# Crossbar transposes, a lag of three blocks and a new VectorE order in a windowed-attention and highway kernel

## Chip, cores, metric

One core of one Trainium2 chip. The metric is the device time of one execution in microseconds; each kernel is run several times and the fast runs are compared. A "span" in a profile is the time from the first to the last instruction and is some 1.7 to 2.4 us shorter than the device time of the same run.

## The reference

Four sequences of 768 tokens, eight heads of 64: every query attends to the 128 last positions and to the first four ("sinks"). The result, as 3072 tokens of 512 features, goes through a highway layer.

```python
keep = (pos[None, :] < 4) | ((rel >= 0) & (rel < 128))
scores = np.where(keep, q @ k.T / 8, -1e9)
x = softmax(scores) @ v                       # [3072, 512]
H = np.maximum(x @ w_h, 0.0)
T = 1.0 / (1.0 + np.exp(-(x @ w_t + b_t)))
out = T * H + (1.0 - T) * x
```

## The kernel before

It works in 24 blocks of 128 tokens, six to a sequence (a "batch" below). Per block TensorE makes transposes of q and k (`tp`), window scores (`sps`), attention output (`av`), transposes of x (`xtp`) and the two highway products (`tps`, `hps`). Once in two blocks it makes sink scores (`sk`). ScalarE does the exponentials (`e`, `es`), copies and the tanh (`u`). VectorE multiplies the masks in (`e`), and does `kT`, `rec`, `xh` (x, normalised), `dd`, `ee`, `otok`. All q, k and v loads are issued by GpSimd and cast fp32 to fp16 on the way. (`dd`, `ee`, `otok` are the three steps of the highway sum; PSUM, below, is the memory that TensorE writes its results to, HBM the memory off the cores.)

```python
AHEAD = 8
x_pool  = tile_pool(name="p_x", bufs=4)
av_ps   = tile_pool(name="ps_av", bufs=1, space=PSUM)
m_ps    = tile_pool(name="ps_m", bufs=2, space=PSUM)   # tp, sk, tps and hps share these two
...
def stage_T(n):                          # q, k of block n to [feature, token]
    ...
    nc.scalar.copy(out=qT, in_=tp[:, 0:NHP, :])
    nc.vector.tensor_copy(out=kT, in_=tp[:, NHP:2 * NHP, :])
def stage_sink_setup(b):                 # once a batch: ten small SBUF-to-SBUF copies
    for hh in range(2):
        nc.sync.dma_start(out=ks3[...], in_=kT[rows, :, 0:NSINK])
    for h in range(H):
        nc.sync.dma_start(out=vs_bd[b % 2][r:r + NSINK, ...], in_=vt[0:NSINK, ...])
def stage_X(n):
    xtp = av_ps.tile([P, NOC, P], FP16, tag="av")
    for j in range(NOC):
        nc.tensor.transpose(xtp[:, j, :], xh[:, 2 * j:2 * j + 2, :], ident)
    nc.scalar.copy(out=xT, in_=xtp)
...
for i in range(-2, NB + 1):              # cut to its order; s = i + 1
    stage_sink(i)                        # blocks 2 and 4 of a batch
    stage_S(s); stage_A(i)               # scores of the next block; av, rec, xh
    stage_T(i + 2); stage_sink_setup(...)
    load(i + 2 + AHEAD); load_v(i + 2 + AHEAD)      # GpSimd's queue
    stage_mask(s)
    stage_Mt(i - 1); stage_X(i)
    stage_Mh(i - 1)                      # hps, then dd, ee, otok one after the other
```

The softmax here doesn't subtract the row's maximum and nothing guards it: scores larger than these inputs give would overflow.

## Time and profile before

| | before |
|---|---|
| device time, median of 3 | 136.59 us |
| VectorE busy, whole span | 108.5 us (80%) |
| one batch of six blocks, steady | 28.1 us |
| last q, k or v load issued | about 80 us |
| q, k loads, issue to landing, median | 7.3 to 7.4 us |

A line of the profile's first page: busy microseconds, share of the span and instructions of each engine (PE is TensorE, PEld its weight loads, DVE VectorE, ACT ScalarE, POOL GpSimd).

```profile
PE 117.1 (87%) x1312; PEld 73.6 (55%) x1312; DVE 108.5 (80%) x230; ACT 90.4 (67%) x129; POOL 65.7 (49%) x81
```

The windows view, one row for each of two batches. Its columns are the stretch and its length, then the busy time and instruction count of TensorE, its weight loads, VectorE, ScalarE and GpSimd, then granted clock, DMA share and GB/s.

```profile
24.20:52.50 28.30, 27.21 (x330) 17.54 (x329) 25.79 (x48) 22.18 (x32) 24.70 (x29) 1.00 2.28 173
52.50:80.60 28.10, 27.01 (x330) 17.37 (x328) 25.83 (x49) 22.18 (x32) 21.64 (x25) 1.00 2.09 189
```

VectorE is busy 92% of such a stretch. The chain of waits shows what that means in one block (start, length, what):

```profile
43.46 0.70 DVE dd L313
...
44.26 0.70 DVE ee L316
...
44.98 0.69 DVE otok L319
45.67 0.13 DVE rec L275
...
45.83 0.69 DVE xh L277
46.52 0.38 DVE kT L186
46.89 1.20 DVE e L247 x2
48.09 0.62 DVE dd L313
```

From dd to dd it is VectorE alone, 4.6 us. Operations that wait for their predecessor (dd to ee, 0.80 us start to start) cost more than independent ones (the two masks, 0.60 each).

The xh of blocks 6, 12, 18 (left out here) and 23 in the timeline of VectorE (start, duration, engine, line, operation, out<-in):

```profile
45.83 0.69 DVE L277 TENSOR_TENSOR xh<-av,rec 128x512 f16<-128x512 f32 x1
73.95 0.69 DVE L277 TENSOR_TENSOR xh<-av,rec 128x512 f16<-128x512 f32 x1
...
125.14 0.69 DVE L277 TENSOR_TENSOR xh<-av,rec 128x512 f16<-128x512 f32 x1
```

A batch is 28.1 us (73.95 - 45.83); after the last block's xh come 9.8 us of drain (134.9 - 125.14).

### The profile page before, as it was taken

The numbers are of one execution on the slowest core, as the hardware profiler recorded it, in microseconds if no ns is written. First come the engines' busy times: TensorE is split into PE (matmuls) and PEld (weight loads), VectorE is DVE, ScalarE is ACT, GpSimd is POOL, SyncE is SP. The second block draws the span as 40 slices with busy tenths as digits, with TensorE's granted clock in tenths as the row PEclk, the third lists the DMA queues.
The fourth block names the chain that finished last, engine by engine and source line by source line (L and its number), as shares of the span: only waits on it lengthen the run. The fifth ranks groups of instructions, "written<-read, shape, count | busy, mean of one in ns | idle before, by whom it ended". The sixth has DMA issues, their size and how long they took to land.

```text
span 134.9 us, 3378 instructions
## 1 busy us (share of the span) xinstructions
PE 117.1 (87%) x1312; PEld 73.6 (55%) x1312; DVE 108.5 (80%) x230; ACT 90.4 (67%) x129; POOL 65.7 (49%) x81
## 2 busy tenths in 40 slices
PE   6657939999999899999999899999998999999720
PEld 2225625856864466567565557656653685665300
DVE  6153724789988999899898998998989998999590
ACT  3054843779775977977777788779767977973310
POOL 6999747889897789979489370000000000000000
PEclk9999995999999999999999999999999999999996
DMA  0999999999999999999999999122011101101111
GB/s 4 111 123 127 160 188 160 155 181 171 154 198 191 196 151 148 152 195 240 192 194 179 193 194 176 38 80 80 6 78 78 63 19 78 78 5 78 78 78 78
DMA packets 81841, 17.02 MB, mean 126 GB/s; under 512 B 77729, under 2 KB 78753, under 8 KB 81826
## 3 DMA queue, kind: packets, MB, share of 16 engines
q0 software_dynamic: 75936, 10.49, 116.0%
q1 hardware_dynamic: 5890, 6.33, 14.6%
q8 instruction: 10, 0.16, 0.5%
q14 instruction: 5, 0.04, 0.1%
HBM read 20.97 MB, written 6.29 MB: 202 GB/s over the span
## 4 chain that ended last, share of the span: by engine, by line
DVE 33%; PE 32%; ACT 11%; issue 8%; POOL 7%; DMA 6%; DVEq 0%; POOLq 0%
PE hps L310 12%; ACT e L234 7%; DMA ksd<-in_k_dram 6%; DVE ee L316 6%; DVE otok L319 6%; DVE dd L313 6%; DVE e L247 5%; DVE xh L277 5%; PE tps L298 4%; PE xtp L286 4%; PE av L262 3%; DVE kT L186 3%; PE sk L211 3%; ACT qT L185 3%; POOL qsd L83 2%
## 5 line engine op out<-in xcount | busy, mean ns | idle before, releaser
L234 ACT ACTIVATE e<-sps,ebias 128x1024 f16<-128x1024 f32 (+1 forms) x48 | 47.4, 1039 | 11.2 <-PE sps L231 6.0
L298 PE MATMUL tps<-wt_sb,xT 128*128 128x512 f16 x96 | 25.5, 390 | 0.0
L310 PE MATMUL hps<-wh_sb,xT 128*128 128x512 f16 x96 | 24.7, 379 | 0.7
L83 POOL DMA_DIRECT2D qsd<-in_q_dram x24 | 21.6, 900 | 4.7 <-DMA wh_sb<-in_moe_w_h_dram 1.0
L84 POOL DMA_DIRECT2D ksd<-in_k_dram x24 | 21.4, 893 | 3.1 <-PE tp L182 1.3
L262 PEld LDWEIGHTS <-e 128*128 128x128 f16 x352 | 19.8, 98 | 3.2 <-issue 0.4
L301 ACT ACTIVATE u<-tps 128x512 f16<-128x512 f32 x24 | 14.4, 600 | 9.5 <-PE tps L298 9.5
L247 DVE TENSOR_TENSOR e<-e,mask 128x1024 f16<-128x1024 f16 x32 | 20.5, 682 | 0.0
L185 ACT COPY qT<-tp 128x512 f16<-128x512 f16 x24 | 14.0, 585 | 9.6 <-PE tp L182 9.6
L313 DVE SCALAR_TENSOR_TENSOR dd<-hps,xh 128x512 f16<-128x512 f32 x24 | 16.5, 688 | 4.1 <-PE hps L310 4.1
L186 DVE COPY kT<-tp 128x512 f16<-128x512 f16 x24 | 10.1, 423 | 11.7 <-ACT qT L185 11.7
L316 DVE SCALAR_TENSOR_TENSOR ee<-u,dd 128x512 f16<-128x512 f16 x24 | 16.6, 692 | 2.5
L319 DVE SCALAR_TENSOR_TENSOR otok<-xh,ee 128x512 f32<-128x512 f16 x24 | 16.6, 692 | 0.8
L277 DVE TENSOR_TENSOR xh<-av,rec 128x512 f16<-128x512 f32 x24 | 16.6, 691 | 0.8
L231 PE MATMUL sps<-qT,kT 64*128 64x128 f16 x352 | 15.4, 227 | 2.1 <-DVE kT L186 1.1
L231 PEld LDWEIGHTS <-kT 64*128 64x128 f16 x352 | 10.7, 98 | 9.5 <-issue 6.6
L288 ACT COPY xT<-xtp 128x512 f16<-128x512 f16 x24 | 14.0, 583 | 1.1 <-PE xtp L286 0.9
L298 PEld LDWEIGHTS <-xT 128*128 128x128 f16 x96 | 9.6, 100 | 9.1 <-issue 0.8
L310 PEld LDWEIGHTS <-xT 128*128 128x128 f16 x96 | 9.3, 98 | 8.6 <-issue 1.5
L286 PEld LDWEIGHTS <-xh 128*128 128x128 f16 x96 | 6.4, 101 | 13.4 <-DVE xh L277 11.2
L286 PE MATMUL xtp<-ident,xh 128*128 128x128 f16 x96 | 9.9, 228 | 3.8 <-DVE xh L277 3.8
L180 PE MATMUL tp<-ident,qsd 128*128 128x128 f16 x96 | 10.0, 231 | 2.4 <-DMA qsd<-in_q_dram 2.3
(88 smaller groups left out, 152.9 us busy)
## 6 DMA issues: line engine op xcount, KB each, us to landing
out_dram<-otok SPq DMA_DIRECT2D x24, 256.0 KB
qsd<-in_q_dram POOLq DMA_DIRECT2D x24, 128.0 KB, 7.3
ksd<-in_k_dram POOLq DMA_DIRECT2D x24, 128.0 KB, 7.4
wt_sb<-in_moe_w_t_dram POOLq DMA_DIRECT2D x1, 512.0 KB, 8.4
wh_sb<-in_moe_w_h_dram POOLq DMA_DIRECT2D x1, 512.0 KB, 10.1
v_91<-in_v_dram POOLq DMA_DIRECT2D x3, 128.0 KB, 8.0
v_92<-in_v_dram POOLq DMA_DIRECT2D x3, 128.0 KB, 6.1
v_93<-in_v_dram POOLq DMA_DIRECT2D x2, 128.0 KB, 8.0
```

Of the source, the lines that this page charges most:

```text
L83: nc.gpsimd.dma_start(out=qsd, in_=q[b, :, rows, :].transpose([1, 0, 2]))
L231: nc.tensor.matmul(sps[:, hh, o:o + P], lhsT=kk[rows, hp, :], rhs=qT[rows, hp, :], start=True, stop=True)
L234: nc.scalar.activation(out=e.rearrange("p a b c d -> p a (b c d)"), in_=sps[:, :, 0:2 * np_ * P], func=AF.Exp, bias=ebias, scale=SCALE)
L247: nc.vector.tensor_tensor(out=ev, in0=ev, in1=m.unsqueeze(1).to_broadcast([P, 4, np_ * P]), op=ALU.mult)
L262: nc.tensor.matmul(av[:, g, 2 * hl + hh, 0:_AVN], lhsT=es[g][:, hh, hl, pc, :], rhs=vt[:, 65 * h:65 * h + _AVN], start=first, stop=False, ...
L277: nc.vector.tensor_tensor(out=xh, in0=avh[:, :, 0:D], in1=rec.unsqueeze(2).to_broadcast([P, H, D]), op=ALU.mult)
L286: nc.tensor.transpose(xtp[:, j, :], xh[:, 2 * j:2 * j + 2, :], ident)
L298: nc.tensor.matmul(tps, lhsT=xT[:, kc, :], rhs=wt_sb[:, kc, :], start=False, stop=(kc == NOC - 1))
L310: nc.tensor.matmul(hps, lhsT=xT[:, kc, :], rhs=wh_sb[:, kc, :], start=(kc == 0), stop=(kc == NOC - 1))
L313: nc.vector.scalar_tensor_tensor(out=dd, in0=hps, scalar=0.0, in1=xh, op0=ALU.max, op1=ALU.subtract)
L316: nc.vector.scalar_tensor_tensor(out=ee, in0=u, scalar=1.0, in1=dd, op0=ALU.add, op1=ALU.mult)
L319: nc.vector.scalar_tensor_tensor(out=otok, in0=xh, scalar=2.0, in1=ee, op0=ALU.mult, op1=ALU.add)
```

## The change

Its intent is to relieve the two busiest engines. x is transposed by the DMA crossbar instead of TensorE and ScalarE, so the highway layer runs three blocks behind to hide the transfer. The kT copy moves to ScalarE, as part of one copy of q and k. VectorE's operations are interleaved so that none directly follows one that it needs. The ten small sink copies become two VectorE copies, one product on VectorE, and one small load by GpSimd, straight from v in HBM.

```diff
-    x_pool = ... bufs=4;  td_pool = ... bufs=3;  NV = AHEAD + 3
+    x_pool = ... bufs=7;  td_pool = ... bufs=4;  NV = AHEAD + 4
-        nc.scalar.copy(out=qT, in_=tp[:, 0:NHP, :])
-        nc.vector.tensor_copy(out=kT, in_=tp[:, NHP:2 * NHP, :])
+        nc.scalar.copy(out=qk, in_=tp)
+    def load_sinks(b):
+        nc.gpsimd.dma_start(out=vs_c[b % 2][:, 0:D], in_=v[b, :, 0:4, :])
     def stage_sink_setup(b):
-        (ten nc.sync.dma_start of ks and vs)
+        nc.vector.tensor_copy(out=ks3[...], in_=kT[rows, :, 0:NSINK])      # twice
+        nc.vector.tensor_tensor(out=vs_bd[...], in0=vs_c[b % 2]..., in1=bdm..., op=ALU.mult)
     def stage_X(n):
-        (four nc.tensor.transpose and a nc.scalar.copy)
+        nc.sync.dma_start_transpose(out=xT, in_=xh.rearrange("p h d -> p (h d)"))
+    LAG = 3
+        for i in range(-2, NB + LAG + 1):        # s = i + 1, m = i - LAG
+            stage_sink(i); stage_S(s); stage_exp(s, 0); stage_T(i + 2); stage_T_copy(i + 2)
+            if (i + 2) % NSC == 0: load_sinks((i + 2) // NSC)
+            load(i + 2 + AHEAD); load_v(i + 2 + AHEAD)
+            stage_exp(s, 1)
+            stage_dd(m - 1); stage_mask(i, 1); stage_ee(m - 1); stage_mask(s, 0)
+            stage_Mt(m); stage_A(i)              # A: av, rec
+            stage_out(m - 1); stage_xh(i); stage_X(i)
+            if i % NSC == 0: stage_sink_setup(i // NSC)
+            stage_Mh(m)
```

(Conditions at the ends of the loop are cut.)

More of the change, by code (lines that the diff above doesn't have):

```diff
@@ L66 @@
     r_pool = ctx.enter_context(tc.tile_pool(name="p_r", bufs=3))
-    x_pool = ctx.enter_context(tc.tile_pool(name="p_x", bufs=4))
-    td_pool = ctx.enter_context(tc.tile_pool(name="p_td", bufs=3))
+    x_pool = ctx.enter_context(tc.tile_pool(name="p_x", bufs=7))
+    td_pool = ctx.enter_context(tc.tile_pool(name="p_td", bufs=4))
     o_pool = ctx.enter_context(tc.tile_pool(name="p_o", bufs=4))
@@ L72 @@
     m_ps = ctx.enter_context(tc.tile_pool(name="ps_m", bufs=2, space=bass.MemoryType.PSUM))
-    NV = AHEAD + 3
+    NV = AHEAD + 4
     v_ring = [const.tile([P, VW], FP16, tag=f"v{i}", name=f"v{i}") for i in range(NV)]
@@ L111 @@
     wt_sb = const.tile([P, NOC, DM], FP16, tag="wt")
+    bdm = const.tile([P, H], FP32, tag="bdm")
+    nc.vector.memset(bdm, 1.0)
     with tc.manual_schedule(engines={ENG.Pool}):
@@ L132 @@
         nc.gpsimd.dma_start(out=wh_sb, in_=moe_w_h.rearrange("(kc p) of -> p kc of", p=P))
+        nc.gpsimd.affine_select(
+            out=bdm, in_=bdm, compare_op=ALU.is_ge, fill=0.0,
+            base=0, pattern=[[-4, H]], channel_multiplier=1)
+        nc.gpsimd.affine_select(
+            out=bdm, in_=bdm, compare_op=ALU.is_ge, fill=0.0,
+            base=NSINK - 1, pattern=[[4, H]], channel_multiplier=-1)
     bt32 = const.tile([1, DM], FP32, tag="bt32")
@@ L143 @@
     mask1 = const.tile([P, 2, P], FP16, tag="mask1", name="mask1")
-    ks_bd, vs_bd = [], []
+    ks_bd, vs_c, vs_bd = [], [], []
     for i in range(2):
-        t = const.tile([P, NHP * 160], FP16, tag=f"ks{i}", name=f"ks{i}")
+        t = const.tile([P, NHP * 136], FP16, tag=f"ks{i}", name=f"ks{i}")
         nc.vector.memset(t, 0.0)
         ks_bd.append(t)
+        t = const.tile([4 * H, 65], FP16, tag=f"vc{i}", name=f"vc{i}")
+        nc.vector.memset(t[:, D:D + 1], 2.0)
+        vs_c.append(t)
         t = const.tile([P, 2, 4, 65], FP16, tag=f"vs{i}", name=f"vs{i}")
@@ L170 @@
     qkT = {}
+    tp_of = {}
+    sps_of = {}
     e_of = {}
     es_of = {}
+    av_of = {}
+    dd_of = {}
+    ee_of = {}
+    hps_of = {}
     xh_of = {}
@@ L182, in stage_T, with stage_T_copy @@
             nc.tensor.transpose(tp[:, NHP + j, :], ksd[:, 2 * j:2 * j + 2, :], ident)
-        qT = qkT_pool.tile([P, NHP, P], FP16, tag="qT", name="qT")
-        kT = qkT_pool.tile([P, NHP, P], FP16, tag="kT", name="kT")
-        nc.scalar.copy(out=qT, in_=tp[:, 0:NHP, :])
-        nc.vector.tensor_copy(out=kT, in_=tp[:, NHP:2 * NHP, :])
-        qkT[n] = (qT, kT)
+        qk = qkT_pool.tile([P, 2 * NHP, P], FP16, tag="qkT", name="qkT")
+        qkT[n] = (qk[:, 0:NHP, :], qk[:, NHP:2 * NHP, :])
+        tp_of[n] = (qk, tp)
+    def stage_T_copy(n):
+        qk, tp = tp_of.pop(n)
+        nc.scalar.copy(out=qk, in_=tp)
+    def load_sinks(b):
+        nc.gpsimd.dma_start(out=vs_c[b % 2][:, 0:D], in_=v[b, :, 0:4, :])
     def stage_sink_setup(b):
         _, kT = qkT[b * NSC]
-        ks3 = ks_bd[b % 2].rearrange("p (a b) -> p a b", b=160)
+        ks3 = ks_bd[b % 2].rearrange("p (a b) -> p a b", b=136)
         for hh in range(2):
             rows = slice(64 * hh, 64 * hh + 64)
-            nc.sync.dma_start(out=ks3[rows, :, 4 * hh:4 * hh + NSINK],
-                              in_=kT[rows, :, 0:NSINK])
-        vt = v_ring[(b * NSC) % NV]
-        for h in range(H):
-            r = 32 * (h // 2) + 4 * (h % 2)
-            nc.sync.dma_start(out=vs_bd[b % 2][r:r + NSINK, h // 4, h % 4, :],
-                              in_=vt[0:NSINK, 65 * h:65 * h + 65])
+            nc.vector.tensor_copy(out=ks3[rows, :, 4 * hh:4 * hh + NSINK],
+                                  in_=kT[rows, :, 0:NSINK])
+        nc.vector.tensor_tensor(
+            out=vs_bd[b % 2][0:4 * H].rearrange("p g h e -> p (g h) e"),
+            in0=vs_c[b % 2].unsqueeze(1).to_broadcast([4 * H, H, 65]),
+            in1=bdm[0:4 * H].unsqueeze(2).to_broadcast([4 * H, H, 65]), op=ALU.mult)
     def stage_sink(n):
@@ L222, in stage_S @@
         es = []
+        sps_of[n] = []
         for g in range(2):
@@ L232, in stage_S, with stage_exp, stage_mask @@
                                          rhs=qT[rows, hp, :], start=True, stop=True)
-            e = e_pool.tile([P, 2, 2, np_, P], FP16, tag="e", name="e")
-            nc.scalar.activation(out=e.rearrange("p a b c d -> p a (b c d)"),
-                                 in_=sps[:, :, 0:2 * np_ * P], func=AF.Exp,
-                                 bias=ebias, scale=SCALE)
-            es.append(e)
-        e_of[n] = (es, np_)
-    def stage_mask(n):
+            sps_of[n].append(sps)
+            es.append(e_pool.tile([P, 2, 2, np_, P], FP16, tag="e", name="e"))
+        e_of[n] = (es, np_)
+    def stage_exp(n, g):
+        es, np_ = e_of[n]
+        nc.scalar.activation(out=es[g].rearrange("p a b c d -> p a (b c d)"),
+                             in_=sps_of[n][g][:, :, 0:2 * np_ * P], func=AF.Exp,
+                             bias=ebias, scale=SCALE)
+    def stage_mask(n, g):
         c = n % NSC
@@ L244, in stage_mask @@
             c, mask.rearrange("p a b -> p (a b)"))
-        for e in es:
-            ev = e.rearrange("p a b c d -> p (a b) (c d)")
-            nc.vector.tensor_tensor(
-                out=ev, in0=ev, in1=m.unsqueeze(1).to_broadcast([P, 4, np_ * P]),
-                op=ALU.mult)
+        ev = es[g].rearrange("p a b c d -> p (a b) (c d)")
+        nc.vector.tensor_tensor(
+            out=ev, in0=ev, in1=m.unsqueeze(1).to_broadcast([P, 4, np_ * P]),
+            op=ALU.mult)
     def stage_A(n):
@@ L275, in stage_A, with stage_xh @@
         nc.vector.reciprocal(out=rec.unsqueeze(2), in_=avh[:, :, 64:65])
+        av_of[n] = (avh, rec)
+    def stage_xh(n):
+        avh, rec = av_of.pop(n)
         xh = x_pool.tile([P, H, D], FP16, tag="xh", name="xh")
@@ L283, in stage_X @@
         xh = xh_of[n]
-        xtp = av_ps.tile([P, NOC, P], FP16, tag="av", name="xtp")
-        for j in range(NOC):
-            nc.tensor.transpose(xtp[:, j, :], xh[:, 2 * j:2 * j + 2, :], ident)
         xT = x_pool.tile([P, NOC, P], FP16, tag="xT", name="xT")
-        nc.scalar.copy(out=xT, in_=xtp)
+        nc.sync.dma_start_transpose(out=xT, in_=xh.rearrange("p h d -> p (h d)"))
         xT_of[n] = xT
@@ L305, in stage_Mh @@
         xT = xT_of.pop(n)
-        xh = xh_of.pop(n).rearrange("p h d -> p (h d)")
-        u = u_of.pop(n)
         hps = m_ps.tile([P, DM], FP32, tag="m", name="hps")
@@ L311, in stage_Mh, with x_flat, stage_dd, stage_ee @@
                              start=(kc == 0), stop=(kc == NOC - 1))
+        hps_of[n] = hps
+    def x_flat(n):
+        return xh_of[n].rearrange("p h d -> p (h d)")
+    def stage_dd(n):
         dd = td_pool.tile([P, DM], FP16, tag="dd", name="dd")
-        nc.vector.scalar_tensor_tensor(out=dd, in0=hps, scalar=0.0, in1=xh,
+        nc.vector.scalar_tensor_tensor(out=dd, in0=hps_of.pop(n), scalar=0.0, in1=x_flat(n),
                                        op0=ALU.max, op1=ALU.subtract)
+        dd_of[n] = dd
+    def stage_ee(n):
         ee = td_pool.tile([P, DM], FP16, tag="ee", name="ee")
-        nc.vector.scalar_tensor_tensor(out=ee, in0=u, scalar=1.0, in1=dd,
+        nc.vector.scalar_tensor_tensor(out=ee, in0=u_of.pop(n), scalar=1.0, in1=dd_of.pop(n),
                                        op0=ALU.add, op1=ALU.mult)
+        ee_of[n] = ee
+    def stage_out(n):
         otok = o_pool.tile([P, DM], FP32, tag="otok", name="otok")
-        nc.vector.scalar_tensor_tensor(out=otok, in0=xh, scalar=2.0, in1=ee,
+        nc.vector.scalar_tensor_tensor(out=otok, in0=x_flat(n), scalar=2.0, in1=ee_of.pop(n),
                                        op0=ALU.mult, op1=ALU.add)
+        del xh_of[n]
         nc.sync.dma_start(out=out[n * P:(n + 1) * P, :], in_=otok)
+    LAG = 3
+    def done(n):
+        return 0 <= n < NB
     with tc.manual_schedule(engines={ENG.PE, ENG.DVE, ENG.Activation}):
-        for i in range(-2, NB + 1):
-            s = i + 1
-            if 0 <= i < NB and i % NSC >= 2 and i % 2 == 0:
+        for i in range(-2, NB + LAG + 1):
+            s, m = i + 1, i - LAG
+            if done(i) and i % NSC >= 2 and i % 2 == 0:
                 stage_sink(i)
-            if 0 <= s < NB:
+            if done(s):
                 stage_S(s)
-            if 0 <= i < NB:
-                stage_A(i)
+                stage_exp(s, 0)
             if i == -2:
@@ L335 @@
                 stage_T(i + 2)
+                stage_T_copy(i + 2)
                 if (i + 2) % NSC == 0:
-                    stage_sink_setup((i + 2) // NSC)
+                    load_sinks((i + 2) // NSC)
             if i == -2:
@@ L346 @@
                     load_v(n)
-            if 0 <= s < NB:
-                stage_mask(s)
-            if 0 <= i - 1 < NB:
-                stage_Mt(i - 1)
-            if 0 <= i < NB:
+            if done(s):
+                stage_exp(s, 1)
+            if done(m - 1):
+                stage_dd(m - 1)
+            if done(i):
+                stage_mask(i, 1)
+            if done(m - 1):
+                stage_ee(m - 1)
+            if done(s):
+                stage_mask(s, 0)
+            if done(m):
+                stage_Mt(m)
+            if done(i):
+                stage_A(i)
+            if done(m - 1):
+                stage_out(m - 1)
+            if done(i):
+                stage_xh(i)
                 stage_X(i)
-            if 0 <= i - 1 < NB:
-                stage_Mh(i - 1)
+            if done(i) and i % NSC == 0:
+                stage_sink_setup(i // NSC)
+            if done(m):
+                stage_Mh(m)
 _INS = ['q', 'k', 'v', 'n_sink', 'window', 'moe_w_h', 'moe_w_t', 'moe_b_t']
```

## The prediction

> **What bounds it now.** In the timeline, a batch of six blocks takes 28.1 us (24.2 to 52.5 us, 52.5 to 80.6, 80.6 to 108.8). VectorE is busy 92% there, the matmul row 96%, ScalarE 78%. The chain of waits alternates between two kinds of block. In one, VectorE goes round without a gap in 4.55 us (43.46 to 48.01): dd, ee, otok, rec, xh, kT, two masks; an operation that depends on the previous one starts up to 0.11 us after its end, an independent one starts 0.08 us before it (0.61 apart instead of 0.72 to 0.80). In the other, with sink scores, hps, sk, es, both exps, qT and kT follow each other in about 5 us. Loads keep the DMA engines full to 84 us but run ahead of use.
>
> **What the change does, per block.** VectorE loses the kT copy (0.42 us) and the dependent gaps: dd, mask, ee, mask, rec, otok, xh at independent distances come to 3.8 us (was 4.55), plus about 0.8 us once a batch for the sinks (was ten small DMAs). TensorE loses the x transposes (0.34 to 0.40 us). ScalarE swaps two 0.58 us copies for one of 1024 columns, about 1.0 us by the page's per-column slope. SyncE gains 24 crossbar transposes of 128 KB.
>
> **How much is on the path.** By engine time TensorE would need about 4.2 us a block, so 10% looks possible. I expect less, because the order creates a new ring. The matmul PSUM pool has two buffers. In the changed kernel's listing tps waits in every steady block for VectorE: it takes the buffer of the previous hps, which dd now frees only after rec, otok and xh. Ring, from durations of before: start of av to rec 1.24 (1.0 without sinks), rec 0.12, otok 0.61, xh 0.61, dd 0.69, wake-up 0.06, tps five matmuls 1.08: 4.41 us. Where a sink stage comes in, tp waits for es in the same buffer: about 4.6. After a batch's first block the sink set-up lies inside the ring: about 4.6. Sum 26.8 us a batch against 28.1, minus 5%, some 4 us over three batches. The first six blocks wait for loads either way (gain about 0). The drain grows by about 2.5 us: three highway blocks remain after the last av instead of one, plus a transpose landing. Net span 133 to 135 against 134.9.
>
> **DMA.** Between xh and its tps lie about 9.7 us. The Trainium skill, "VectorE: DVE Perf Modes", section The three transpose paths, gives 1309 ns for one 128x128 crossbar transpose against 390 on TensorE; no trace here shows one yet. Four make about 5 us (estimate from that page), beside loads that themselves take 7.3 us to land. I expect it to fit.
>
> **Predicted: 135.6 us, 8 in 10 between 130.5 and 143. Faster by over 2%: 0.30; within: 0.45; slower: 0.25.**
>
> **Right or wrong in the profile.** Right: VectorE near 95 us busy; steady batches near 26.8 us; the chain of waits runs av, rec, otok, xh, dd, tps and back; tps waits for dd; VectorE idles before rec. Wrong: if batches take 25 us, the ring is shorter than I think; if TensorE waits for xT, the transposes land too late.
>
> **What would make it wrong.** Transposes above 9.7 us in the loaded stage, or slowing the loads so that tp waits for them (slower). A ring that overlaps more than I sum, giving TensorE's 4.2 us a block: about 128 us.

## The result, and the profile after

| | before | changed |
|---|---|---|
| device time, median | 136.72 us (4 runs) | 152.17 us (4 runs, 150.82 to 153.11) |
| ratio of fast runs | | 1.110 (95%: 1.101 to 1.120) |
| span of the profiled run | 134.9 us | 151.4 us |

A ratio, here and below, is the mean time of one kernel's fast runs over that of the other's of the same rounds, so it is not quite the ratio of the medians. The profiled run of the changed kernel counts as slow (1.5% above its fastest run); the reading below does not rest on that, since fast runs of later kernels (e3, e6) show the same kind of wait.

First page and windows view of the changed kernel, the same lines as above (the stretches are the gap, and the batch of blocks 12 to 17):

```profile
PE 111.8 (74%) x1216; PEld 71.6 (47%) x1216; DVE 98.8 (65%) x223; ACT 87.0 (57%) x105; POOL 68.5 (45%) x87
```
```profile
47.20:63.00 15.80, 0.67 (x12) 0.51 (x9) 0.38 (x4) 2.97 (x3) 9.29 (x11) 0.65 2.46 154
92.40:119.00 26.60, 24.98 (x302) 16.44 (x302) 23.07 (x47) 21.29 (x28) 1.46 (x2) 1.00 0.95 131
```

TensorE, VectorE and ScalarE have less work than before (GpSimd slightly more), and the batch of blocks 12 to 17 takes 26.6 us instead of 28.1. But from 47.2 to 63.0 us TensorE and VectorE do almost nothing. The waits view (who waited for whom: total, times, longest) names it:

```profile
PE tps L322 <- DVE dd L343: 19.5, 6, 16.4
DVE vs_169 L220 <- DMA vc_167<-in_v_dram: 15.4, 1, 15.4
DVE vs_163 L220 <- DMA vc_161<-in_v_dram: 7.5, 1, 7.5
```

And the timelines of VectorE and, below it, of GpSimd give the reason:

```profile
46.61 0.69 DVE L306 TENSOR_TENSOR xh<-av,rec 128x512 f16<-128x512 f32 x1
47.22 0.34 DVE L218 COPY ks_165<-qkT 64x16 f16<-64x16 f16 x2
62.96 0.69 DVE L220 TENSOR_TENSOR vs_169<-vc_167,bdm 32x520 f16<-32x520 f16 x1 [15.40 <-DMA vc_167<-in_v_dram]
```
```profile
53.56 0.88 POOL L84 DMA_DIRECT2D ksd<-in_k_dram  x1 [3.35 <-DMA v_101<-in_v_dram]
54.42 0.89 POOL L91 DMA_DIRECT2D v_92<-in_v_dram  x1
56.62 0.58 POOL L210 DMA_DIRECT2D vc_167<-in_v_dram  x1 [1.31 <-DMA ksd<-in_k_dram]
```

VectorE, which also works strictly in order, reaches the sink product of block 6 at 47.6 us. Its operand `vc_167` is 4 KB, but the instruction that fetches it stands in GpSimd's queue behind the loads of blocks up to 13 (`v_92` is the v of block 13), because the program loads eight blocks ahead. GpSimd, which itself waits for earlier loads on the way (the brackets), gets there at 56.62 us and the bytes land at 62.9. Nothing behind the product can run: no dd, hence no tps, hence no av. TensorE also comes out of the gap at a lower granted clock: 0.65 on average in the gap, 0.50 from 63 to 66 us, 0.63 from 66 to 70 and 1.00 from 70 us on. The four products of the first tps after the gap take 1.71 us in the chain of waits, those of the next 0.86.

The xh lines of blocks 6, 12, 18 and 23:

```profile
46.61 0.69 DVE L306 TENSOR_TENSOR xh<-av,rec 128x512 f16<-128x512 f32 x1
90.80 0.68 DVE L306 TENSOR_TENSOR xh<-av,rec 128x512 f16<-128x512 f32 x1
117.36 0.68 DVE L306 TENSOR_TENSOR xh<-av,rec 128x512 f16<-128x512 f32 x1
138.82 0.68 DVE L306 TENSOR_TENSOR xh<-av,rec 128x512 f16<-128x512 f32 x1
```

One batch takes 44.2 us, the next 26.6. So 17.6 us are lost in one place, 15.4 of them in the wait and some 2 in the slow restart, and the change gains 1.5 us in an undisturbed batch.

### The profile page after: what moved, and what is told of

It reads as the page before. It is cut to its first block, busy times and chain, and to the rows that moved or that the text cites. A ratio compares the mean times of both kernels' runs of the same rounds, so it can differ in the third digit from the quotient of the medians.

```text
span 151.4 us, 3124 instructions
## 1 busy us (share of the span) xinstructions
PE 111.8 (74%) x1216; PEld 71.6 (47%) x1216; DVE 98.8 (65%) x223; ACT 87.0 (57%) x105; POOL 68.5 (45%) x87
## 4 chain that ended last, share of the span: by engine, by line
PE 42%; DVE 23%; DMA 19%; POOL 8%; issue 4%; ACT 1%; DVEq 0%; POOLq 0%
PE tps L324 11%; PE av L287 10%; DMA ksd<-in_k_dram 9%; DVE otok L355 7%; DVE dd L343 6%; DMA vc_161<-in_v_dram 6%; DVE xh L306 5%; PE hps L334 4%; DMA vc_167<-in_v_dram 4%; PE tps L322 4%; PE sps L254 3%; POOL qsd L83 3%; PE sk L233 3%; POOL ksd L84 2%; PE av L293 2%
## 5 line engine op out<-in xcount | busy, mean ns | idle before, releaser
L262 ACT ACTIVATE e<-sps,ebias 128x1024 f16<-128x1024 f32 (+1 forms) x48 | 50.0, 1048 | 9.1 <-PE sps L254 9.0
L207 ACT COPY qkT<-tp 128x1024 f16<-128x1024 f16 x24 | 24.2, 1009 | 10.3 <-PE tp L200 10.3
L287 PEld LDWEIGHTS <-e 128*128 128x128 f16 x352 | 22.9, 103 | 9.8 <-DVE e L272 4.3
L322 PE MATMUL tps<-bt_152,ones_row 128*128 128x512 f16 x24 | 9.3, 386 | 20.1 <-DVE dd L343 19.5
L272 DVE TENSOR_TENSOR e<-e,mask 128x1024 f16<-128x1024 f16 x32 | 21.9, 684 | 1.6 <-ACT e L262 1.3
L254 PE MATMUL sps<-qkT 64*128 64x128 f16 x352 | 16.0, 231 | 3.7 <-ACT qkT L207 2.6
L254 PEld LDWEIGHTS <-qkT 64*128 64x128 f16 x352 | 11.3, 100 | 10.8 <-issue 8.7
L300 DVE RECIPROCAL rec<-av 128x8 f32<-128x8 f32 x24 | 5.0, 208 | 16.3 <-PE av L293 11.8
L236 ACT ACTIVATE es<-sk,ebias 128x256 f16<-128x256 f32 x8 | 3.8, 474 | 13.4 <-PE sk L233 13.4
L220 DVE TENSOR_TENSOR vs_169<-vc_167,bdm 32x520 f16<-32x520 f16 x2 | 1.4, 688 | 15.4 <-DMA vc_167<-in_v_dram 15.4
```

What stands on the lines that cost most here:

```text
L207: nc.scalar.copy(out=qk, in_=tp)
L254: nc.tensor.matmul(sps[:, hh, o:o + P], lhsT=kk[rows, hp, :], rhs=qT[rows, hp, :], start=True, stop=True)
L262: nc.scalar.activation(out=es[g].rearrange("p a b c d -> p a (b c d)"), in_=sps_of[n][g][:, :, 0:2 * np_ * P], func=AF.Exp, bias=ebias, sc ...
L272: nc.vector.tensor_tensor(out=ev, in0=ev, in1=m.unsqueeze(1).to_broadcast([P, 4, np_ * P]), op=ALU.mult)
L287: nc.tensor.matmul(av[:, g, 2 * hl + hh, 0:_AVN], lhsT=es[g][:, hh, hl, pc, :], rhs=vt[:, 65 * h:65 * h + _AVN], start=first, stop=False, ...
```

## The experiments

Two theories at this point. **Queue**: the place of the small load in GpSimd's in-order queue is the cause. **Crossbar**: the transposes slow the big loads (GpSimd reached the v of block 13 at 54.4 us, the kernel before at 46.0), and the sink wait was only where that showed first. Each of these experiments also ran the kernel before on the same chip; e1 to e4 share one set of it (median 136.54 us), e5 to e8 another (137.47). All results were correct.

| run | what | median us | ratio to before (95%) |
|---|---|---|---|
| e1 | sink loads early, by SyncE | 134.98 | 0.989 (0.982 to 0.995) |
| e2 | e1, x transposed on TensorE | 137.20 | 1.006 (0.998 to 1.013) |
| e3 | changed kernel, x transposed on TensorE | 145.42 | 1.064 (1.056 to 1.072) |
| e4 | e1, otok moved out of the ring | 131.34 | 0.960 (0.950 to 0.969) |
| e5 | before, plus dead crossbar transposes | 146.49 | none (3 of 4 runs slow) |
| e6 | before, with the sink values of the change | 143.99 | 1.045 (1.040 to 1.049) |
| e7 | changed kernel, sink loads early, by GpSimd | 138.50 | 1.007 (1.002 to 1.011) |
| e8 | e4, first 8 blocks transposed on TensorE | 130.42 | 0.948 (0.944 to 0.953) |

### e1: the sink loads first, on SyncE

```diff
-        nc.gpsimd.dma_start(out=vs_c[b % 2][:, 0:D], in_=v[b, :, 0:4, :])   # in the loop
+    for b in range(B):                                                      # before the loop
+        t = const.tile([4 * H, 65], FP32, tag=f"vc{b}", name=f"vc{b}")
+        nc.vector.memset(t[:, D:D + 1], 2.0)
+        nc.sync.dma_start(out=t[:, 0:D], in_=v[b, :, 0:4, :])
```

(Cut: the product then reads `vs_c[b]` instead of `vs_c[b % 2]`.)

Expected: 

> Changed kernel, but the four small sink-value loads are issued by SyncE at the very start, in fp32 (VectorE reads them as fp32), instead of by GpSimd among the big loads. Theory Q (queue position): VectorE's waits of 15.4 us and 7.5 us for the sink values are the whole loss, because each small load stood in GpSimd's in-order queue behind the loads of blocks far ahead. Then no such wait is left, the batches take 26.6 us from the first on (as between 92.5 and 119.0 us of the changed kernel), and the time is 152.2 - 16.1 - 2.7 = about 133.5 us (131 to 136.5). Theory X (crossbar): the transposes make the q, k and v loads slow, and the sink wait was only where it showed; then TensorE waits for qsd, ksd or xT instead, and the time stays above 142 us.

Measured: 134.98 us, and no wait for the sink values in the waits view. The xh lines of blocks 6, 12, 18 and 23, from VectorE's timeline of e1:

```profile
45.91 0.68 DVE L306 TENSOR_TENSOR xh<-av,rec 128x512 f16<-128x512 f32 x1
72.48 0.68 DVE L306 TENSOR_TENSOR xh<-av,rec 128x512 f16<-128x512 f32 x1
99.04 0.68 DVE L306 TENSOR_TENSOR xh<-av,rec 128x512 f16<-128x512 f32 x1
120.48 0.68 DVE L306 TENSOR_TENSOR xh<-av,rec 128x512 f16<-128x512 f32 x1
```

Both batches take 26.6 us. The Queue theory holds, the Crossbar theory as stated falls: the crossbar is still there. Only the sink loads were changed (place, engine and type; e7 separates these), and 17 us came back. The first wait, of 7.5 us in block 0, was worth little: block 6's xh came only 0.7 us earlier, because the first blocks wait for their q and k anyway.

### e2: e1 without the crossbar

```diff
-        nc.sync.dma_start_transpose(out=xT, in_=xh...)        # at the end of block i
+        (four nc.tensor.transpose into av_ps, nc.scalar.copy) # after the scores of block i + 2
```

Expected: 

> As e1, but x is transposed on TensorE again (one block late, after the score matmuls, copied by ScalarE), lag 3 kept. Theory Q: the crossbar is nearly neutral: within 3% of e1 (ScalarE gets 0.58 us a block back, about 4.5 us of work, and TensorE 0.34), so 133 to 138 us. Theory X: at least 5% faster than e1.

Measured: 137.20 us, 1.6% above e1. The crossbar is worth about 2 us once nothing else stalls (against this one place for the TensorE transposes), and it does delay the loads: their median landing is 7.1 to 7.2 us here and 10.2 us for ksd in e1, and the last ksd is issued at 76.0 us here and at 95.8 in e1. In e1 they still come in time.

### e3: the change without the crossbar, sink loads left where they are

The edit of e2, on the changed kernel.

Expected: 

> Changed kernel with x transposed on TensorE as in e2, the sink loads left in GpSimd's queue. Theory Q: the stall at block 6 stays, though it may be shorter: in the trace of before, GpSimd reaches the same place in its load sequence (after block 13's v) at 46 to 47 us, a load lands 7 to 8 us later, VectorE needs it at about 47: so a wait of 6 to 8 us if the crossbar alone made the loads later, 15 us if it did not; time 142 to 152 us. Theory X: the wait vanishes and the time is below 138 us.

Measured: 145.42 us. A line of the waits view of e3, and its two waits in the timeline of VectorE, in block 0 and in block 6:

```profile
DVE vs L220 <- DMA vc<-in_v_dram: 10.2, 2, 6.1
22.83 0.69 DVE L220 TENSOR_TENSOR vs<-vc,bdm 32x520 f16<-32x520 f16 x1 [6.13 <-DMA vc<-in_v_dram]
52.26 0.69 DVE L220 TENSOR_TENSOR vs<-vc,bdm 32x520 f16<-32x520 f16 x1 [4.09 <-DMA vc<-in_v_dram]
```

The sink load of block 6 is issued at 45.41 us instead of 56.62, and the wait there is 4.1 us instead of 15.4 (6 to 8 were expected). So the position in the queue is enough for a stall, and the crossbar, by slowing the loads ahead of it (k loads issued from 40 to 47 us took 13.5 us to land in the changed kernel and 7.4 here, medians), made it 11 us longer. In whole times, the position costs 8.2 us without the crossbar (145.42 against 137.20 in e2) and 17.2 with it (152.17 against 134.98 in e1). The second theory described an amplifier: without the place in the queue there is no stall (e1), but about half of its cost comes with the crossbar.

### e4: otok out of the ring

```diff
+            stage_dd(m - 1); stage_out(m - 2); stage_mask(i, 1); stage_ee(m - 1); stage_mask(s, 0)
-            stage_dd(m - 1); stage_mask(i, 1); stage_ee(m - 1); stage_mask(s, 0)
             stage_Mt(m); stage_A(i)
-            stage_out(m - 1); stage_xh(i)
+            stage_xh(i)
```

(on e1; one more buffer in `x_pool` and `td_pool`, one more turn of the loop)

Expected: 

> As e1, but otok is moved out of the ring: VectorE does rec, xh, dd and then the otok of the block before. If the ring av, rec, otok, xh, dd, tps (4.41 us) sets the pace, taking 0.61 us out and paying 0.12 us for rec before xh makes it 3.9 us, below TensorE's own 4.2 us; where sink scores come in, 4.6 us stays. Then a batch takes about 25.7 us instead of 26.6 and the time is about 3 us (2%) below e1. If the ring is not the limit, the time equals e1 within 0.5%.

Measured: 131.34 us, 2.7% below e1 and 4% below the kernel before. This tests the pace of the undisturbed part. The chain of waits of e1, one block of it:

```profile
80.37 0.40 PE av L287 x8
...
81.43 0.03 DVE rec L300
...
81.57 0.63 DVE otok L355
82.20 0.60 DVE xh L306
82.80 0.61 DVE dd L343
...
83.45 0.38 PE tps L322
83.83 0.86 PE tps L324 x4
84.69 0.40 PE av L287 x8
```

(Of an operation that overlaps its successor the chain counts only the part up to that one's start, hence 0.03 us of rec.) It is a ring: av, rec, otok, xh, dd, tps, av, 4.32 us (80.37 to 84.69), though TensorE and VectorE are each busy less than that (24.9 and 23.0 us of a batch, so 4.2 and 3.8 a block). tps needs one of the two PSUM buffers, and the one that comes free is that of the last hps, when dd has read it. otok has no place in that dependency; it is in the ring only because VectorE works in order. In e4 the same stretch of the chain is TensorE alone:

```profile
53.01 0.40 PE av L287 x8
...
53.52 0.40 PE av L287 x8
53.91 0.11 PE av L293
54.03 0.86 PE hps L334 x4
54.89 0.55 PE sps L254 x16
55.44 0.33 PE tp L201 x4
55.77 0.22 PE tp L203 x4
56.00 0.22 PE tps L322
56.21 0.86 PE tps L324 x4
57.08 0.40 PE av L287 x8
```

That is 4.07 us from one av to the next (53.01 to 57.08), with no gap. A batch takes 25.3 us. It breaks the rule of the change once (xh directly follows rec, start to start 0.24 us instead of 0.12) and is faster for it: an order is good by what it takes out of the longest ring, not by the number of its small gaps.

### e5: what the transposes cost the loads

```diff
         nc.scalar.copy(out=xT, in_=xtp)
+        dead = x_pool.tile([P, NOC, P], FP16, tag="dead", name="dead")
+        nc.sync.dma_start_transpose(out=dead, in_=xh.rearrange("p h d -> p (h d)"))
```

(on the kernel before)

Expected: 

> The kernel before, plus one crossbar transpose of every xh into a tile that nobody reads (its result stays right). It measures what the transposes cost the loads. If they take DMA time from the q, k and v loads, the last ksd is issued later than the 79.5 us of before, towards the 93 to 96 us of the kernels with the crossbar, and the landings take over 7.4 us; as the loads run ahead of use here, the time should move by under 2% (135.5 to 139 us). If the transposes do not disturb the loads, the last issue stays within 2 us of 79.5.

Measured: the last ksd is issued at 94.9 us instead of 79.5 and the median landings are 8.6 to 9.6 us: the transposes do take DMA time from the loads. The time, 143.04 to 148.74 us, missed the expectation. The waits of the profiled run, itself a slow one (146.85 us), suggest why it is not a clean measure of the time: the dead transposes hold the four xh buffers, and in SyncE's in-order queue they stand among the ten sink copies. VectorE waited 3.3 us for an out transfer and then 2.4 us for a dead transpose, around the third batch's set-up; block 6's xh was already 4.0 us late (49.86 against 45.83), which stays unexplained. Three of the four runs count as slow, so the runs spread too much for a ratio.

### e6: the queue position alone, in the kernel before

```diff
-        (eight nc.sync.dma_start of vs)
+        nc.gpsimd.dma_start(out=vs_c[b % 2][:, 0:D], in_=v[b, :, 0:4, :])   # same place as in the change
+        nc.vector.tensor_tensor(out=vs_bd..., in0=vs_c..., in1=bdm..., op=ALU.mult)   # end of block 0 of a batch
```

Expected: 

> The kernel before, with only the sink values as in the change: a small load in GpSimd's queue at the same place, spread by one VectorE product at the end of each batch's first block. Theory Q (queue position alone is enough): VectorE waits about 7 us in block 6 (issue at 46 to 47 us, landing 7 us later, needed at 46.6) and a little in block 0; time 142 to 147 us. Rival (it takes the crossbar or the lag as well): under 139 us.

Measured: 143.99 us, 4.5% slower than before, without crossbar, without lag, without the new order. The waits view of e6:

```profile
DVE vs L213 <- DMA vc<-in_v_dram: 8.1, 2, 6.1
```

VectorE waits 8.1 us for the sink values: 6.1 us in the first batch and 2.0 us in the second. The split is not the one expected (about 7 us in the second batch), because here the set-up comes later relative to the loads; the sum is. Not all of the loss is the wait: VectorE has one product more (0.68 us) in each batch, and from block 12 to 18, where nothing waits for sink values, e6 takes 29.0 us (xh at 78.92 and 107.94) instead of 28.1.

### e7: the same engine and type, only early

```diff
         load_v(1)
+        for b in range(B):
+            nc.gpsimd.dma_start(out=vs_c[b][:, 0:D], in_=v[b, :, 0:4, :])
```

(on the changed kernel, the loads in the loop removed)

Expected: 

> The changed kernel, its four sink loads still issued by GpSimd and still cast to fp16, but all four right after the loads of block 1. Theory Q: no wait of VectorE for the sink values in block 6, so within 3 us of e1: about 0.6 us each of GpSimd's time delays the first blocks, 135 to 138.5 us. Rival (e1 was fast because it used another queue or fp32, not because it was early): above 142 us.

Measured: 138.50 us, at the edge of what was expected, and no wait for the sink values. So it was neither fp32 nor SyncE that cured e1. The early place on GpSimd's own queue costs more than SyncE's: by the two ratios (1.007 and 0.989) e7 is 1.8% or about 2.5 us above e1, about four issues of 0.6 us. All of it lies before block 6, whose xh comes at 48.99 us instead of 45.91; the batch after that takes 26.6 us in both.

### e8: crossbar only where the loads are not in the way

In e4 the chain shows TensorE waiting for a ksd that lands at 103.7 us: two xh there are 6.0 us apart (100.52 and 106.50) instead of 4.3. e8 transposes blocks 0 to 7 on TensorE, when it waits for loads anyhow.

```diff
+            if done(i - 1) and i - 1 < 8: stage_X_pe(i - 1)     # four transposes, nc.scalar.copy
-                stage_X(i)
+                if i >= 8: stage_X(i)                           # crossbar
```

Expected: 

> As e4, but the first 8 blocks are transposed on TensorE (ScalarE copies), where both engines still wait for loads; the crossbar does the rest. In e4 the last loads come too late (TensorE waits for ksd at 103.7 us, some 2 us). Eight transposes less, at about 0.85 us of DMA time each (last loads of e1 and e2 20 us apart over 24 transposes), bring the loads some 7 us forward, so that wait should go: about 129.5 us, 1 to 2% below e4. If ScalarE's copies cost more than the loads gain: equal to e4 or up to 2% above.

Measured: 130.42 us, ratio 0.948 to its own set of the kernel before, against 0.960 for e4 in the other set. The two xh that were 6.0 us apart are 4.3 apart here (100.45 and 104.78). The intervals meet at 0.95, so that e8 is better than e4 is likely but not shown. The last load is issued at about 79 us again instead of 94.6. Both beat both kernels of the study.

## Why the prediction was wrong

The step that failed is "plus about 0.8 us once a batch for the sinks (was ten small DMAs)". It costed the work on VectorE (0.34 us for the two copies and 0.69 for the product are measured, so about right) and forgot that the product now has an operand from HBM, fetched by an instruction that stands in GpSimd's queue after loads eight blocks ahead. In the kernel before, the sink values came out of a tile that was already on the chip. "Loads ... run ahead of use" was true of the big loads and just for that reason false of the small one: it joins the end of the line. The order of GpSimd's instructions and the issue times of the kernel before were there to be read, and would have given a wait of some us: the expectation of e3, worked out from them, said 6 to 8 us in block 6, and 4.1 came; the crossbar's part, 11 us on top, was not to be had from the trace of before.

The terms of the sum, in e1, where that step is mended, against the kernel before:

| term | predicted | measured (before to e1) |
|---|---|---|
| first blocks | about 0 | +0.1 us (xh of block 6: 45.83 to 45.91) |
| one batch | 28.1 to 26.8 | 28.1 to 26.6 us |
| blocks 6 to 23 | -4 us | -4.7 us (79.3 to 74.6) |
| drain after the last xh | +2.5 us | +2.5 us (9.8 to 12.3) |
| span | 133 to 135 | 132.8 us |
| changed kernel: sink stall | 0 | +17.6 us (batch of 44.2 us), +0.7 at the start |

- The ring was right in its members, its cause and its length (4.41 us predicted, 4.32 measured in a block without sink scores), and e4 shows that it was the limit. That the batch came so close (26.8 predicted, 26.6 measured) is partly luck: after the block with the set-up the next xh came 5.07 us later (45.91 to 50.98) where 4.6 was predicted, and the last step of the batch took 3.69 us (68.79 to 72.48), shorter than any ring in the prediction, so two errors cancel.
- VectorE's busy time was predicted near 95 us and is 98.8 us (99.4 in e1): independent operations follow each other in 0.60 us, as assumed; I did not break the 4 us down.
- "I expect it to fit": the transposes landed 2.4 us after issue at best, 7.1 us in the median and 9.0 us at most, within the 9.7 us allowed (in e1 TensorE waited for one once, 1.2 us). The Trainium skill, "VectorE: DVE Perf Modes", section The three transpose paths, gives 1309 ns for one 128x128 transpose by the crossbar; four of them one after the other, as the prediction took it, would be 5.2 us, so once the loads are over it is faster than that estimate from the page (the last five took 2.4 to 2.5 us) and beside the loads slower.
- "Slowing the loads" was listed as a risk, and came true: it cost little in e1, about 1.7 us in e4, and some 11 us of the 15.4 us stall in the changed kernel. The Trainium skill, "DMA: Bandwidth & Descriptors", section Issuing engines are not separate DMA queues, says that transfers of all issuing engines share the same 16 DMA engines; e1 against e2 agrees, with the last ksd issue 20 us later over 24 transposes.

Open: how the DMA engines share their time between a transpose and the loads (why single loads took up to 13.5 us just before the gap) is not settled by these runs. Nor was the other end of the wait tested: the product stands at the end of a batch's block 0 on VectorE, but the first to read its result is the av of block 2 (`c >= 2` in stage_A). In e3 the bytes were there at 52.3 us, and e2, which is e3 without the wait, has the xh of block 8 at 55.9; there a later place for the product might have hidden the wait.

## What to carry to other kernels

When a change moves an operand from on-chip memory to a new load, ask where in the issuing engine's queue the new instruction stands, not how many bytes it moves: a 4 KB load behind a prefetch of eight blocks is as late as the eighth block. If it is needed early, issue it early. And for the order of an in-order engine, write down the ring through the scarcest buffer first, then take out of it what does not belong there.

## What the Trainium skill lacked or had wrong

- "DMA: Bandwidth & Descriptors", section Issuing engines are not separate DMA queues, says that issuing from several engines only saves the initiation time, "which is usually small relative to the DMA itself". Here the place in the issuing engine's queue decided over 17.6 us (changed kernel against e1), and e7 shows that an early place on the same engine removes the stall. A warning about small loads behind prefetches is missing.
- The same page's section on the anatomy of a GpSimd-issued DMA calls descriptor generation "small, variable". In the changed kernel's trace GpSimd is busy about 0.9 us for each 128 KB load and still about 0.6 us for one of 4 KB.
- The same page's section DMA Transpose (X-bar) has no latency for an SBUF-to-SBUF transpose beside other traffic. For 128x512 fp16 it is 2.4 us at best, 7.1 us in the median here, and SyncE's own issue takes 1.2 us; 24 of them moved the last load by about 20 us, some 0.8 us each.
- "VectorE: DVE Perf Modes", section The DRAIN you can't avoid, gives no cost for an operation that directly follows the one it needs: 0.80 us from start to start (dd to ee) against 0.60 to 0.61 us for independent operations of 0.68 to 0.69 us.
